# The opening re-planned with measured durations, and a tile's score stage joined to the preceding tile's output stage

## The chip, the cores and the metric

The kernel runs on one core of one Trainium2 chip. The metric is the time of one execution on the device in microseconds (us); of several runs the median is taken. The profile is one further execution, with its own time.

## The reference

Chunked attention, then two feed-forward layers over its output (4608 tokens of 512 features):

```python
def _attn_ref(q, k, v):                  # 8 x 8 x 576 x 64, chunks of 64
    scores = scale * np.matmul(q_c, k_c.transpose(0, 1, 2, 4, 3))
    scores = scores - np.max(scores, axis=-1, keepdims=True)
    attn = np.exp(scores)
    attn = attn / (np.sum(attn, axis=-1, keepdims=True) + 1e-09)
    out = np.matmul(attn, v_c)
def _moe_ref(x, w_in, w_out, alpha):     # 512 -> 2048 -> 512
    h = x @ w_in
    g = np.maximum(h, 0.0) + alpha * np.minimum(h, 0.0)
    return g @ w_out
def _moe2_ref(x, w_in, w_out):
    h = x @ w_in
    g = np.where(h > 0.0, h, np.exp(np.minimum(h, 0.0)) - 1.0)
    return g @ w_out
```

All inputs are float32; the weights are handed over as 64-bit words and are turned into float32 on the chip.

## The kernel before

The 4608 tokens are 9 blocks of 512, and a block is 4 attention tiles of 128 tokens (36 tiles, numbered t). Each float32 operand of the two layers is split into a high and a low part, and a product is three TensorE matmuls (high times high, high times low, low times high).

**A tile's attention** is three stages on TensorE, with work of other engines between them:
- S(t), `att_s` (L227): 16 matmuls for the scores, of q and the block-diagonal k (`kbd`). Behind it `softmax` on VectorE (maximum and subtraction, L238 and L240), `exponent` on ScalarE (L245), `normalize` on VectorE (L249 to L251) and `weigh` (L255; on VectorE for tiles 0 to 3, on GpSimd, POOL in the profile, for the others).
- T(t), `att_pt` (L266): 4 transposes of the weights `p`. Behind it `put_pt` (L272): two ScalarE copies into the block-diagonal buffer `pbd`, of which there is one.
- V(t), `att_av` (L280): 16 matmuls for the output of the tile, of v and `pbd`. Behind it `put_x` (L292), a ScalarE copy into `xf`; a block's four tiles are split into `xhi` and `xlo` (L342, L346; for block 0 L511 and L515).

The scores, the transposes and the outputs share two PSUM buffers (`ps_a`); in the first 12 stages the four accumulators of the second product serve too.

**A layer's step** is F(j,f), `first` (L366): 12 matmuls of 128x512 for slice f (of 16) of the hidden features of block j, into one of two PSUM buffers `h`; the activation and the split of its result follow on ScalarE and VectorE; and `second` (L438): 12 matmuls of 128x512 that add that slice into the accumulators `acc`.

**Three parts follow one another.** `start()`, the opening, plans tasks by a list scheduler: each task has an engine, a cost and a due time; of those whose predecessors are issued it takes the one that could begin first by its own sums, and among those within SLACK the one due first. What it takes is issued at once, so this sets the order of every engine's queue, SyncE's DMA queue (SP) among them. In the opening the weights are prepared piece by piece (32 pieces of the first layer: load, abs L125, low L150, clamp L132 and L136, join L143, add L155 on POOL, hi L159, lo L163 on POOL), tiles 0 to 11 are attended, and F(0,·), F(1,·) run, then F(2,·) in turn with second(0,·). Results g of blocks 0 to 2 are stored to memory (L569) and loaded again for `second`. MERGE is the number of slices of block 0 that come before F(1,0). `catch_up()` then runs the second product of blocks 1 and 2, and `rest()` the remaining blocks of the first layer and then all of the second layer: each step is one `first`, at most one attention stage of the next block, and one `second`. `att_order(j)` gives the stages of a block's four tiles in the order "S0 S1 T0 S2 V0 T1 S3 V1 T2 - V2 T3 - V3", one a step, "-" being a step without one. `att_stage` issues a stage; what follows it on other engines is put into `later` and issued by `flush()` at the next stage or `second`. The first layer ends near 920 us; behind that there is no attention left.

Of the kernel before, what the change touches and what calls it, by code (L numbers as in the profile page):

```python
# [22 lines left out]
START = 25.0  # L23
STEP = 3.6
LAG = 0.3
SLACK = 0.2
MERGE = 8
# [12 lines left out]
def tile_chunk_attention_prelu_elu(  # L40
# [420 lines left out]
    def start():  # L461
# [8 lines left out]
        def add(name, engine, cost, due, do, *after):  # L470
            def issue():
                got[name] = do()

            tasks[name] = (engine, cost, due, issue, after)
# [3 lines left out]
        for i in range(2 * KFF):  # L478
            name, f = ("in", "out")[i // KFF], i % KFF
            due = START + STEP * i - 6 if i < KFF else START + STEP * (KFF + f + 4)  # L480
            held_by = ()
            if name == "out" and f in held:
                held_by = (held[f],)
# [9 lines left out]
            add(("load", i), "dma", 1.5, due, w_load, ("add", i - 3))  # L493
            add(("abs", i), "act", 0.6, due, w_abs, ("load", i), ("lo", i - 2), ("add", i - 1))
            add(("low", i), "act", 0.6, due, w_low, ("abs", i))
            add(("clamp", i), "dve", 1.0, due, w_clamp, ("abs", i))
            add(("join", i), "dve", 0.8, due, w_join, ("clamp", i))
            add(("add", i), "pool", 1.3, due, w_add, ("join", i), ("low", i))
            add(("hi", i), "act", 0.6, due, hi, ("add", i), ("lo", i - 1), *held_by)
            add(("lo", i), "pool", 1.3, due, lo, ("hi", i))  # L500
# [3 lines left out]
        stages = [(int(op[1]), "STV".index(op[0])) for op in "S0 S1 T0 S2 V0 T1 S3 V1 T2 V2 T3 V3".split()]  # L504
        for j in range(1, AHEAD):
            stages += [op for op in att_order(j) if op]
# [10 lines left out]
        def user(n):  # L517
            t, k = stages[n]
            return (("max", t), ("put", t), ("y" if t < TPB else "x", t))[k]

        for n, (t, k) in enumerate(stages):
            j = t // TPB
            due = 4 + 2.5 * t if j == 0 else START + STEP * (KFF * (j - 1) + 3 * (t % TPB) + 1)
            free = n - (5 if n < 12 else 2)
            need = [user(free)] if free >= 0 else []
            need += [(("k", t),), (("weigh", t),), (("put", t), ("v", t))][k]
            if n:
                need.append(("STV"[stages[n - 1][1]], stages[n - 1][0]))
            bank = banks[n % 5] if n < 12 else banks[0]
            add(("STV"[k], t), "pe", (1.1, 0.5, 1.1)[k], due, lambda t=t, k=k, bank=bank: ATT[k][0](t, *bank), *need)  # L530
            if k == 0:
                add(("k", t), "dma", 1.5, due - 3, lambda t=t: load_qk(t), ("S" if place(t) == 0 else "V", t - PLACES))
                add(("v", t), "dma", 0.7, due, lambda t=t: load_v(t), ("V", t - PLACES), ("k", t))
                add(("max", t), "dve", 1.35, due, lambda t=t: softmax(t, got["S", t]), ("S", t), ("T", t - 2))
                add(("exp", t), "act", 0.55, due, lambda t=t: exponent(t), ("max", t))
                add(("norm", t), "dve", 1.1, due, lambda t=t: normalize(t), ("exp", t))
                add(("weigh", t), "dve" if j == 0 else "pool", 0.6 if j == 0 else 1.1, due, lambda t=t: weigh(t), ("norm", t))
            if k == 1:
                add(("put", t), "act", 1.0, due, lambda t=t: put_pt(t, got["T", t]), ("T", t), ("V", t - 1))
            if k == 2 and j == 0:  # L540
                add(("x", t), "act", 0.5, due, lambda t=t: x0(t), ("V", t))
                add(("y", t), "dve", 0.7, due, lambda t=t: y0(t), ("x", t))
            if k == 2 and j > 0:
                add(("x", t), "act", 0.5, due, lambda t=t: put_x(t, got["V", t]), ("V", t), *((("xhi", 1, kk) for kk in range(KDM)) if j == 2 else ()), *((("xlo", 1, kk) for kk in range(KDM)) if j == 2 else ()))
        n = AHEAD * TPB
        add(("k", n), "dma", 1.5, 1e3, lambda n=n: load_qk(n), ("S", n - PLACES))
        add(("v", n), "dma", 0.7, 1e3, lambda n=n: load_v(n), ("V", n - PLACES), ("k", n))
        for j in range(1, AHEAD):
            due = START + STEP * (KFF * j - 2)
# [3 lines left out]
            for kk in range(KDM):  # L553
                def x_first(j=j, kk=kk):
                    if kk == 0:
                        x_parts(1, j, spare=(j == 1))
                    x_hi(1, j, kk)

                add(("xhi", j, kk), "act", 0.55, due, x_first, *ready, ("xhi", j, kk - 1))
                add(("xlo", j, kk), "dve", 0.65, due, lambda j=j, kk=kk: x_lo(1, j, kk), ("xhi", j, kk))  # L560


        firsts = [(0, f) for f in range(KFF)]
        for f in range(KFF):
            firsts.insert(MERGE + 2 * f + 1, (1, f)) if MERGE + 2 * f + 1 < len(firsts) else firsts.append((1, f))
        firsts += [(2, f) for f in range(KFF)]
# [4 lines left out]
        for n, (j, f) in enumerate(firsts):  # L571
            due = START + STEP * n if j < 2 else START + STEP * 2 * KFF + 5.2 * f + 2.6
            ready = [("y", t) for t in range(TPB)] if j == 0 else [("xlo", j, kk) for kk in range(KDM)]
            before = [firsts[n - i] if n >= i else (9, 9) for i in range(4)]
            add(("F", j, f), "pe", 2.6, due, lambda j=j, f=f: first(1, j, f), *ready, ("lo", f), ("F", *before[1]), ("parts", *before[2]))
            last = ("store", *before[3 if j < 2 else 2])
            if j < 2:
                add(("parts", j, f), "act", 1.0, due + 3, lambda j=j, f=f: prelu_parts(got["F", j, f]), ("F", j, f), last)
                add(("join", j, f), "dve", 0.7, due + 3, lambda j=j, f=f: prelu_join(f, *got["parts", j, f]), ("parts", j, f))
                add(("store", j, f), "dma", 0.8, due + 3, lambda j=j, f=f: store(j, f, got["parts", j, f][0]), ("join", j, f))  # L580
            else:
                add(("parts", j, f), "dve", 1.4, due + 3, lambda f=f: prelu(f, got["F", 2, f]), ("F", j, f), last)
                add(("store", j, f), "dma", 0.8, due + 3, lambda f=f: store(2, f, got["parts", 2, f]), ("parts", j, f))
        for s in range(KFF + 3):
            j, f = divmod(s, KFF)
            due = START + STEP * 2 * KFF + 5.2 * s
            add(("g", s), "dma", 0.8, due - 12, lambda j=j, f=f: g_load(j, f), ("store", j, f), ("glo", s - 3))
            if s <= KFF:
                add(("ghi", s), "act", 0.55, due - 5, lambda j=j, f=f: g_hi(1, j, f, gl_t[j, f]), ("g", s), ("second", s - 3), ("store", 1, KFF - 1), ("glo", s - 1))
                add(("glo", s), "dve", 0.65, due - 5, lambda j=j, f=f: g_lo(1, j, f, gl_t.pop((j, f))), ("ghi", s))  # L590
            if s < KFF:
                add(("second", s), "pe", 2.6, due, lambda f=f: second(1, 0, f), ("glo", s), ("lo", KFF + f), ("second", s - 1))
        add(("alpha",), "dma", 0.1, 12, lambda: nc.sync.dma_start(out=alpha_sb, in_=alpha))
        add(("neg",), "dve", 0.1, START, lambda: nc.vector.tensor_scalar_mul(neg_alpha, alpha_sb, -1.0), ("alpha",))
        t = tasks["join", 0, 0]
        tasks["join", 0, 0] = (*t[:4], (*t[4], ("neg",)))

        done, free = {}, {}
        while tasks:
            best = None  # L600
            for name, (engine, cost, due, do, after) in tasks.items():
                if any(a in tasks for a in after):
                    continue
                at = max([free.get(engine, 0)] + [done.get(a, 0) + LAG for a in after])
# [6 lines left out]
            done[name] = at + cost + (2.0 if engine == "dma" else 0)  # L611
# [10 lines left out]
    def catch_up():  # L622
# [3 lines left out]
        for s in range(KFF, AHEAD * KFF):  # L626
            j, f = divmod(s, KFF)
            g_ahead(s)
            if s % 2 == 0 and stages:
                att_stage(stages.pop(0))  # L630
# [7 lines left out]
    def rest():  # L638
# [3 lines left out]
        for s, (ph, j, f) in enumerate(steps):  # L642
# [11 lines left out]
            if stages:  # L654
                att_stage(stages.pop(0))
# [62 lines left out]
```

## Time and profile before

| | |
|---|---|
| median of 3 runs | 1716.97 us (1716.6 to 1718.39) |
| the profiled execution, its own time | 1718.72 us |
| its span in the trace | 1716.9 us |
| TensorE (PE) busy | 1684.2 us, 98% |
| VectorE (DVE) / ScalarE (ACT) / GpSimd (POOL) busy | 864.9 / 551.3 / 214.7 us |
| mean granted TensorE clock | 0.995 of full speed |

The page cuts the span into 40 equal slices of 43 us and gives each engine's busy share in tenths; the first slices are the opening. The chain of waits goes back from the last instruction to what released each step. The timeline lists instructions in order of time with the idle time before each and the engine that ended it. PE's busy time counts a matmul from its start to a modelled end, and at half clock for as long as it then took; so a busy PE need not be at its peak.

### The profile page before, as it was taken

How to read it: one execution, taken by the hardware profiler on the slowest of the kernel's cores; microseconds unless marked ns; L12 is line 12 of the kernel's file. 1: busy time of each engine (PE TensorE's matmuls, PEld its weight loads, DVE VectorE, ACT ScalarE, POOL GpSimd, SP SyncE). 2: the span in 40 equal slices, each digit the busy share in tenths (PEclk: the TensorE clock that was granted, in tenths of full speed). 3: DMA queues.
4: the chain of work that ended last, by engine and by line, in shares of the span. 5: the costliest groups of instructions: out<-in, count | busy, mean ns of one | idle time of the engine just before them, and what ended most of it. 6: DMA issues, size and time to landing. Idle time of an engine off the chain costs nothing.

```text
span 1716.9 us, 20822 instructions
## 1 busy us (share of the span) xinstructions
PE 1684.2 (98%) x8208; PEld 1375.8 (80%) x8208; DVE 864.9 (50%) x1317; ACT 551.3 (32%) x937; POOL 214.7 (13%) x176
## 2 busy tenths in 40 slices
PE   6799999999999999999999999999999999999998
PEld 5587888888888888888887888888888888888887
DVE  6868743265655656564435343434343444444443
ACT  4776423222323233322233232322222222222222
POOL 3545410011110211110043000000000000000000
PEclk8999999999999999999999999999999999999999
DMA  7755544333323323320143010101010000000000
GB/s 227 216 171 191 178 134 137 92 123 99 111 93 124 115 76 123 99 86 20 50 129 117 1 49 1 50 0 50 1 45 5 34 16 27 23 19 31 12 14 25
DMA packets 72578, 133.48 MB, mean 78 GB/s; under 512 B 7328, under 2 KB 23712, under 8 KB 71328
## 3 DMA queue, kind: packets, MB, share of 16 engines
q1 hardware_dynamic: 72480, 132.16, 24.0%
q8 instruction: 64, 1.05, 0.3%
q14 instruction: 34, 0.28, 0.1%
HBM read 92.28 MB, written 39.85 MB: 77 GB/s over the span
## 4 chain that ended last, share of the span: by engine, by line
PE 94%; DVE 3%; ACT 1%; DMA 1%; issue 1%; SPq 0%; POOL 0%; DVEq 0%; ACTq 0%; POOLq 0%
PE acc L438 46%; PE h L366 43%; PE x L280 2%; PE s L227 2%; PE pt L266 1%; DVE xlo L346 1%; DVE pos L385 1%; DVE wt L132 0%; SPq L205 0%; ACT pbd L272 0%; DMA out<-k_t 0%; ACT wt L125 0%; DMA out<-q_t 0%; DMA q<-q_t 0%; DVE mx L238 0%
## 5 line engine op out<-in xcount | busy, mean ns | idle before, releaser
L366 PE MATMUL h<-xhi,in 128*128 128x512 f32 x2176 | 714.9, 391 | 2.9 <-POOL in L163 1.3
L366 PEld LDWEIGHTS h<-xhi,in 128*128 128x128 f32 x2176 | 409.2, 188 | 90.9 <-POOL in L163 2.4
L366 PE MATMUL h<-xlo,in 128*128 128x512 f32 x1088 | 424.5, 390 | 1.6 <-DVE xlo L346 1.4
L438 PE MATMUL acc<-ghi,out 128*128 128x512 f32 x1152 | 382.4, 396 | 0.0
L438 PE MATMUL acc<-out,ghi 128*128 128x512 f32 x1152 | 354.6, 389 | 0.0
L413 ACT ACTIVATE ghi<-gf 128x512 fp32r<-128x512 f32 x240 | 151.6, 632 | 481.6 <-DVE gf L394 364.1
L418 DVE TENSOR_TENSOR glo<-gf,ghi 128x512 fp32r<-128x512 f32 x240 | 166.3, 693 | 183.5 <-ACT ghi L413 183.5
L438 PEld LDWEIGHTS acc<-ghi,out 128*128 128x128 f32 x1152 | 216.2, 188 | 52.3 <-issue 8.2
L438 PEld LDWEIGHTS acc<-out,ghi 128*128 128x128 f32 x1152 | 216.2, 188 | 44.8
L366 PEld LDWEIGHTS h<-xlo,in 128*128 128x128 f32 x1088 | 204.8, 188 | 44.8 <-DVE xlo L346 2.9
L404 ACT ACTIVATE gf<-gf 128x512 f32<-128x512 f32 x144 | 91.0, 632 | 454.2 <-DVE gf L403 454.2
L438 PE MATMUL acc<-glo,out 128*128 128x512 f32 x576 | 224.8, 390 | 0.0
L438 PE MATMUL acc<-out,glo 128*128 128x512 f32 x576 | 224.1, 389 | 0.0
L403 DVE TENSOR_SCALAR gf<-h 128x512 f32<-128x512 f32 x144 | 99.4, 691 | 220.3 <-PE h L366 220.3
L391 DVE TENSOR_SCALAR gf<-h,alpha_sb 128x512 f32<-128x512 f32 x112 | 83.2, 743 | 146.8 <-PE h L366 146.8
L405 DVE SCALAR_TENSOR_TENSOR gf<-gf,h 128x512 f32<-128x512 f32 x144 | 99.2, 689 | 109.0 <-ACT gf L404 109.0
L155 POOL TENSOR_TENSOR wt<-wt,w 128x512 int32<-128x512 int32 x64 | 88.8, 1387 | 377.4 <-DVE wt L143 198.9
L438 PEld LDWEIGHTS acc<-out,glo 128*128 128x128 f32 x576 | 108.2, 188 | 22.5
L438 PEld LDWEIGHTS acc<-glo,out 128*128 128x128 f32 x576 | 108.3, 188 | 20.1
L394 DVE SCALAR_TENSOR_TENSOR gf<-h,gf 128x512 f32<-128x512 f32 x112 | 77.4, 691 | 3.8
L418 DVE TENSOR_TENSOR glo<-gl,ghi 128x512 fp32r<-128x512 f32 x48 | 35.7, 743 | 63.0 <-ACT ghi L413 63.0
L255 POOL TENSOR_TENSOR p<-p,sm 128x512 f32<-128x512 f32 x32 | 35.5, 1110 | 213.3 <-DVE sm L251 213.3
(60 smaller groups left out, 1023.2 us busy)
## 6 DMA issues: line engine op xcount, KB each, us to landing
w<-moe_w_in SPq DMA_DIRECT2D x32, 512.0 KB, 4.6
w<-moe_w_out SPq DMA_DIRECT2D x32, 512.0 KB, 3.8
gl<-g SPq DMA_DIRECT2D x48, 256.0 KB, 2.8
mid<-ost SPq DMA_DIRECT2D x36, 256.0 KB, 2.4
xf<-mid SPq DMA_DIRECT2D x9, 1024.0 KB, 5.1
out<-ost SPq DMA_DIRECT2D x36, 256.0 KB, 2.0
g<-pos SPq DMA_DIRECT2D x32, 256.0 KB, 2.7
kbd<-k_t SPq DMA_DIRECT2D x54, 128.0 KB, 2.7
```

What stands on the lines that cost most here:

```text
L155: nc.gpsimd.tensor_tensor(out=t, in0=t, in1=words[:, 0], op=ALU.add)
L227: nc.tensor.matmul(s[par * CH:(par + 1) * CH, hp], qq[:, h * CH:(h + 1) * CH], kbd[place(t)][:, :, h, :], start=True, stop=True,)
L255: (nc.vector if t < TPB else nc.gpsimd).tensor_tensor(out=p_t[t], in0=p_t[t], in1=sm, op=ALU.mult)
L366: nc.tensor.matmul(h, w[:, a], x, start=(kk == 0 and m == 0), stop=(kk == KDM - 1 and m == 2),)
L391: nc.vector.tensor_scalar(out=gf, in0=h, scalar1=0.0, scalar2=alpha_sb[:, f:f + 1], op0=ALU.min, op1=ALU.mult)
L394: nc.vector.scalar_tensor_tensor(out=gf, in0=h, scalar=0.0, in1=gf, op0=ALU.max, op1=ALU.add)
L403: nc.vector.tensor_scalar_min(gf, h, 0.0)
L404: nc.scalar.activation(out=gf, in_=gf, func=AF.Exp)
L405: nc.vector.scalar_tensor_tensor(out=gf, in0=gf, scalar=-1.0, in1=h, op0=ALU.add, op1=ALU.max)
L413: nc.scalar.activation(out=ghi, in_=gf, func=AF.Copy)
L418: nc.vector.tensor_sub(glo, gf, ghi.bitcast(F32))
L438: nc.tensor.matmul(acc[e], l, r, start=(f == 0 and m == 0), stop=(f == KFF - 1 and m == 2))
```

## The change

`COST` gives the planner a duration for each kind of task, in place of numbers beside each task; `START`, `STEP`, the lag and the due times of weights, loads and attention are new; the engines are free for planning at 2.0 (DMA queue), 6.5 (POOL) and 4.0. `MERGE` goes from 8 to 4. Tiles 4 to 7 are staged in the order of block 0, followed by S(8) (`ONE = 2`); from there `att_order` yields a list of stages for each step: T(t), then V(t) with S(t+1) directly behind it, then two steps without any. In the opening such a pair is one PE task (`run`), in `catch_up` and `rest` one call of `att_step`. So S(t+1), that of the next block too, stands in the step of V(t): 27 pairs, of V(8) with S(9) to V(34) with S(35), and S(12) moves from `catch_up` into the opening. What each engine computes is the same.

```diff
-START = 25.0
-STEP = 3.6
-LAG = 0.3
+COST = {
+    "load": 2.25, "k": 2.3, "v": 1.15, "store": 1.1, "g": 1.1, "alpha": 0.1,
+    "abs": 0.7, "low": 0.7, "clamp": 1.05, "wjoin": 0.75, "add": 1.35, "hi": 0.67, "lo": 1.35,
+    "S": 1.23, "T": 0.46, "V": 1.23, "VS": 2.15, "F": 2.72, "second": 2.72,
+    "max": 1.42, "exp": 0.67, "norm": 1.15, "weigh": 0.7, "weigh_pool": 1.3, "put": 1.22,
...
+LAG = 0.12
+LAND = 1.9
 SLACK = 0.2
-MERGE = 8
+START = 33.0
+STEP = 3.0
+
+MERGE = 4
+
+ONE = 2
...
     def att_order(j):
 
-        for op in "S0 S1 T0 S2 V0 T1 S3 V1 T2 - V2 T3 - V3".split():
-            yield (j * TPB + int(op[1]), "STV".index(op[0])) if op != "-" else None
+
+        for t in range(j * TPB, (j + 1) * TPB):
+            yield ((t, 1),)
+            yield ((t, 2), (t + 1, 0)) if t + 1 < NTILE else ((t, 2),)
+            yield ()
+            yield ()
...
-    def att_stage(stage):
-        if stage is None:
-            return
-        t, k = stage
-        pe, post = ATT[k]
-        while (t, k - 1) in later:
+    def att_step(ops):
+        while any((t, k - 1) in later for t, k in ops):
             flush()
-        got = pe(t, ps_a, "a")
+        got = [ATT[k][0](t, ps_a, "a") for t, k in ops]
         flush()
-        load_next(t, k)
-        later[t, k] = lambda: post(t, got)
+        for (t, k), o in zip(ops, got):
+            load_next(t, k)
+            later[t, k] = lambda t=t, k=k, o=o: ATT[k][1](t, o)
...
+        stages = []
+        for j in range(AHEAD):
+            if j < ONE:
+                ops = "S0 S1 T0 S2 V0 T1 S3 V1 T2 V2 T3 V3".split()
+                stages += [(j * TPB + int(op[1]), "STV".index(op[0])) for op in ops]
+                stages += [(ONE * TPB, 0)] * (j == ONE - 1)
+            else:
+                stages += [op for ops in att_order(j) for op in ops]
...
+        def run(units):
+            for n in units:
+                t, k = stages[n]
+                got["STV"[k], t] = ATT[k][0](t, *bank(n))
...
-        done, free = {}, {}
+        done, free = {}, {"dma": 2.0, "pool": 6.5}
```

**On TensorE in the opening, around S(8) and T(8).** Before, from V(7) on (`in_724` and `in_801` are the weights of slices 5 and 6, each F being nine rows):

```order
L280 MATMUL x<-pbd,out_423 64x128 x8
L227 MATMUL s<-kbd_93,q 64x128 x8
L366 MATMUL h<-xhi,in_724 128x512
...
L227 MATMUL s<-out_94,out_629 64x128 x8
L366 MATMUL h<-xhi,in_801 128x512
...
L266 MATMUL pt<-ident,p 128x128 x4
L227 MATMUL s<-out_95,out_711 64x128 x8
```

Now, from F(0,4) on (`in_674`; `in_381` is slice 0, which with `out_718` is F(1,0); `in_1060` slice 11, `in_853` slice 7, `in_1113` slice 12):

```order
L385 MATMUL h<-xhi,in_674 128x512
...
L245 MATMUL s<-kbd_93,q 64x128 x8
L385 MATMUL h<-out_718,in_381 128x512 x3
...
L385 MATMUL h<-xhi,in_1060 128x512
...
L284 MATMUL pt<-ident,p 128x128 x4
L385 MATMUL h<-out_718,in_853 128x512 x3
...
L298 MATMUL x<-pbd,v 64x128 x8
L245 MATMUL s<-out_94,out_634 64x128 x8
L385 MATMUL h<-xhi,in_1113 128x512
```

Between S(8) and T(8) stood two F and S(9); now there stand 14 F, and S(9) has moved behind V(8), with two F between it and T(9).

**On TensorE in `rest`, block 3.** Before, S and V each stand alone between a `first` (h) and a `second` (acc):

```order
L366 MATMUL h<-xhi,in_724 128x512
L227 MATMUL s<-kbd_93,q 64x128 x8
L438 MATMUL acc_3164<-ghi,out_1528 128x512
...
L366 MATMUL h<-xhi,in_801 128x512
L280 MATMUL x<-pbd,v 64x128 x8
L438 MATMUL acc_3164<-ghi,out_1578 128x512
```

Now:

```order
L284 MATMUL pt<-ident,p 128x128 x4
L457 MATMUL acc_3179<-ghi,out_1399 128x512
...
L385 MATMUL h<-xhi,in_613 128x512
L298 MATMUL x<-pbd,v 64x128 x8
L245 MATMUL s<-kbd_93,q 64x128 x8
L457 MATMUL acc_3179<-ghi,out_1504 128x512
```

V and S stand in one stretch, one step (a `second` and a `first`) behind the T of the same tile, where V used to follow its T after two steps.

## Rows read from the trace of the kernel before

**Rows 1.** The page: span, PE's busy line, granted clock in 40 slices, chain by engine

```profile
span 1716.9 us, 20822 instructions
...
PE 1684.2 (98%) x8208; PEld 1375.8 (80%) x8208; DVE 864.9 (50%) x1317; ACT 551.3 (32%) x937; POOL 214.7 (13%) x176
...
PEclk8999999999999999999999999999999999999999
...
PE 94%; DVE 3%; ACT 1%; DMA 1%; issue 1%; SPq 0%; POOL 0%; DVEq 0%; ACTq 0%; POOLq 0%
```

**Rows 2.** Who PE waited for, whole span: us in total, times, longest

```profile
PE s L227 <- DMA q<-q_t: 7.0, 2, 6.2
PE pt L266 <- DVE p L255: 5.8, 2, 4.2
PE pt L266 <- POOL p L255: 5.6, 2, 4.8
PE x L280 <- ACT pbd L272: 4.5, 5, 1.3
```

**Rows 3.** Chain by time, block 3: start us, us, what, count

```profile
352.93 1.02 PE s L227 x16
353.95 2.94 PE acc L438 x12
356.89 2.72 PE h L366 x12
...
378.92 1.02 PE x L280 x16
379.94 2.94 PE acc L438 x12
...
385.61 0.44 PE pt L266 x4
386.05 2.77 PE acc L438 x12
...
391.54 1.02 PE s L227 x16
```

**Rows 4.** Timeline of PE, V(7), S(8), T(8), S(10): start, us, what, count, idle before

```profile
60.69 1.09 PE L280 MATMUL x<-pbd,out 128*64 128x128 f32 x16
61.61 1.04 PE L227 MATMUL s<-kbd,q 128*64 128x128 f32 x16
62.59 0.50 PE L366 MATMUL h<-xhi,in 128*128 128x512 f32 x1
...
76.27 1.12 PE L266 MATMUL pt<-ident,p 128*128 128x128 f32 x4 [4.85 <-POOL p L255]
77.31 1.98 PE L227 MATMUL s<-out,out 128*64 128x128 f32 x16
```

**Rows 5.** Chain by time: F(0,7) at 79 us, and the first second(0,0)

```profile
79.29 4.45 PE h L366 x12
...
166.11 2.72 PE acc L438 x12
```

**Rows 6.** Windows: us, busy by engine, granted clock, DMA share, GB/s

```profile
57.00:85.00 28.00, 21.17 (x137) 15.53 (x136) 23.91 (x36) 18.28 (x34) 15.39 (x12) 0.88 0.70 214
```

**Rows 7.** Timeline of PE: waits at 163 and 252 us

```profile
163.10 0.50 PE L366 MATMUL h<-xhi,in 128*128 128x512 f32 x1 [0.95 <-DVE gf L394]
...
252.40 1.09 PE L227 MATMUL s<-kbd,q 128*64 128x128 f32 x16 [0.72 <-DMA q<-q_t]
```

**Rows 8.** Timeline of PE, S(6)

```profile
42.01 1.09 PE L227 MATMUL s<-out,out 128*64 128x128 f32 x16 [0.63 <-PE pt L266]
```

**Rows 9.** Timeline of POOL, weigh of tiles 6 and 8

```profile
46.63 1.29 POOL L255 TENSOR_TENSOR p<-p,sm 128x512 f32<-128x512 f32 x1 [2.62 <-DVE sm L251]
...
74.85 1.36 POOL L255 TENSOR_TENSOR p<-p,sm 128x512 f32<-128x512 f32 x1 [0.44 <-DVE sm L251]
```

**Rows 10.** Timeline of ScalarE, put_pt behind the T at 385.61

```profile
387.77 1.17 ACT L272 COPY pbd<-pt 64x512 f32<-64x512 f32 x2
```

More of the change, by code (lines that the diff above doesn't have):

```diff
@@ L468, in start, with add, task @@
         tasks, got = {}, {}
-        def add(name, engine, cost, due, do, *after):
+        def add(name, engine, due, do, *after, cost=None):
             def issue():
                 got[name] = do()
-            tasks[name] = (engine, cost, due, issue, after)
+            tasks[name] = (engine, COST[cost or name[0]], due, issue, after)
+        firsts = [(0, f) for f in range(KFF)]
+        for f in range(KFF):
+            firsts.insert(MERGE + 2 * f + 1, (1, f)) if MERGE + 2 * f + 1 < len(firsts) else firsts.append((1, f))
+        firsts += [(2, f) for f in range(KFF)]
+        f_due = {}
+        for n, (j, f) in enumerate(firsts):
+            f_due[j, f] = START + STEP * n if j < 2 else START + STEP * 2 * KFF + 5.44 * f + 2.72
+        f_due[AHEAD, 0] = START + STEP * 2 * KFF + 5.44 * KFF
+        s_due = [START + STEP * 2 * KFF + 5.44 * s for s in range(KFF + 3)]
+        stages = []
[6 more added lines that the diff above has]
+                stages += [op for ops in att_order(j) for op in ops]
+        def task(t, k):
+            return ("V", t - 1) if k == 0 and t > ONE * TPB else ("STV"[k], t)
         held = {6: ("S", 9), 7: ("S", 10), 8: ("S", 11), 9: ("V", 9), 10: ("V", 10), 11: ("V", 11)}
@@ L491, in lo, with bank, user @@
                 w_lo(wt[f"1{name}", f], single.pop(0)[4].bitcast(F32))
[L493 to L500, printed above, removed]
-        banks = [(ps_a, "a"), *((ps_acc, f"acc{e}") for e in range(KDM))]
-        stages = [(int(op[1]), "STV".index(op[0])) for op in "S0 S1 T0 S2 V0 T1 S3 V1 T2 V2 T3 V3".split()]
-        for j in range(1, AHEAD):
-            stages += [op for op in att_order(j) if op]
+            add(("load", i), "dma", due - LOAD_EARLY, w_load, ("add", i - 3))
+            add(("abs", i), "act", due, w_abs, ("load", i), ("lo", i - 2), ("add", i - 1))
+            add(("low", i), "act", due, w_low, ("abs", i))
+            add(("clamp", i), "dve", due, w_clamp, ("abs", i))
+            add(("wjoin", i), "dve", due, w_join, ("clamp", i))
+            add(("add", i), "pool", due, w_add, ("wjoin", i), ("low", i))
+            add(("hi", i), "act", due, hi, ("add", i), ("lo", i - 1), *held_by)
+            add(("lo", i), "pool", due, lo, ("hi", i))
+        banks = [(ps_a, "a"), *((ps_acc, f"acc{e}") for e in range(KDM))]
+        def bank(n):
+            return banks[n % 5] if n < 3 * TPB else banks[0]
+        def user(n):
+            t, k = stages[n]
+            return (("max", t), ("put", t), ("y" if t < TPB else "x", t))[k]
         parts0 = x_parts(1, 0)
@@ L515, in y0 @@
             nc.vector.tensor_sub(parts0[1][:, :, a], got["V", t], parts0[0][:, :, a].bitcast(F32))
-        def user(n):
-            t, k = stages[n]
-            return (("max", t), ("put", t), ("y" if t < TPB else "x", t))[k]
+        def run(units):
+            for n in units:
+                t, k = stages[n]
+                got["STV"[k], t] = ATT[k][0](t, *bank(n))
+            return got["STV"[stages[units[0]][1]], stages[units[0]][0]]
         for n, (t, k) in enumerate(stages):
             j = t // TPB
[L523 to L530, printed above, removed]
-            if k == 0:
[L532 to L537, printed above, removed]
@@ new lines, in start @@
+            due = 4 + 2.5 * t if j == 0 else f_due[j, 0] - ATT_EARLY[j] - ATT_STEP[j] * (TPB - t % TPB)
+            if task(t, k) == ("STV"[k], t):
+                units = [n] + [n + 1] * (n + 1 < len(stages) and task(*stages[n + 1]) == ("STV"[k], t))
+                need = [task(*stages[n - 1])] if n else []
+                for m in units:
+                    free = m - (5 if m < 3 * TPB else 2)
+                    if free >= 0:
+                        need.append(user(free))
+                    need += [[("k", stages[m][0])], [("weigh", t)], [("put", t), ("v", t)]][stages[m][1]]
+                add(task(t, k), "pe", due, lambda units=units: run(units), *need, cost="VS" if len(units) > 1 else None)
@@ new lines, in start @@
+            if k == 0:
+                if t < AHEAD * TPB:
+                    add(("k", t), "dma", due - 3, lambda t=t: load_qk(t), task(t - PLACES, 0 if place(t) == 0 else 2))
+                    add(("v", t), "dma", due, lambda t=t: load_v(t), ("V", t - PLACES), ("k", t))
+                add(("max", t), "dve", due, lambda t=t: softmax(t, got["S", t]), task(t, 0), ("T", t - 2))
+                add(("exp", t), "act", due, lambda t=t: exponent(t), ("max", t))
+                add(("norm", t), "dve", due, lambda t=t: normalize(t), ("exp", t))
+                on = "dve" if t < TPB else "pool"
+                add(("weigh", t), on, due, lambda t=t: weigh(t), ("norm", t), cost="weigh" if on == "dve" else "weigh_pool")
@@ L543, in start @@
+                add(("y", t), "dve", due, lambda t=t: y0(t), ("x", t))
             if k == 2 and j > 0:
[L544 to L547, printed above, removed]
+                parts = [(p, 1, kk) for p in ("xhi", "xlo") for kk in range(KDM)] if j == 2 else ()
@@ L557, in x_first @@
                     x_hi(1, j, kk)
[L559 to L566, printed above, removed]
+                add(("xhi", j, kk), "act", due, x_first, *ready, ("xhi", j, kk - 1))
+                add(("xlo", j, kk), "dve", due, lambda j=j, kk=kk: x_lo(1, j, kk), ("xhi", j, kk))
         def store(j, f, g):
@@ L591, in start @@
             if s < KFF:
[L592 to L596, printed above, removed]
-        done, free = {}, {}
+                add(("second", s), "pe", due, lambda f=f: second(1, 0, f), ("glo", s), ("lo", KFF + f), ("second", s - 1))
@@ L603, in start @@
                     continue
-                at = max([free.get(engine, 0)] + [done.get(a, 0) + LAG for a in after])
+                at = max([free.get(engine, 4.0)] + [done.get(a, 0) + LAG for a in after])
                 if best is None or at < best[0] - SLACK or (at < best[0] + SLACK and due < best[1]):
@@ L610, in start @@
             free[engine] = at + cost
-            done[name] = at + cost + (2.0 if engine == "dma" else 0)
+            done[name] = at + cost + (LAND if engine == "dma" else 0)
     def g_ahead(s):
@@ L629, in catch_up @@
             if s % 2 == 0 and stages:
-                att_stage(stages.pop(0))
+                att_step(stages.pop(0))
             if s == AHEAD * KFF - 2:
@@ L654, in rest @@
             if stages:
-                att_stage(stages.pop(0))
+                att_step(stages.pop(0))
             second(ph, j, f)
```

50 lines of the change are left out of this document (33 added, 17 removed).

## Prediction

> **What bounds the kernel now.** I read the page first: PE is busy for 98% of the span and the chain that ended last is PE for 94%, so the kernel is bound by TensorE, and only two things can shorten it: less time on PE for the same work, or fewer holes in its queue [rows 1]. The granted clock is 9 in every slice but the first, so time that is lost to the clock is lost in the opening [rows 1]. Then the waits of PE, to see where the holes are. Four kinds matter: S for the DMA of q, T for VectorE's `weigh`, T for POOL's `weigh`, V for `put_pt` on ScalarE; their longest are 6.2, 4.2, 4.8 and 1.3 us, and the totals are little more than those, so they are few and in the opening [rows 2]. Last the chain in a steady block, where nothing waits. There I read what a stage costs: a group of 12 big matmuls takes 2.72 us behind another group, but 2.94 behind an S or a V, and 2.77 behind a T [rows 3]. So an S or V of 1.02 us costs 1.24 in all, and a T of 0.44 costs 0.49.
>
> **The pairs.** The trace of before holds V and S side by side once at full clock, in the opening: V(7) begins at 60.69, S(8) at 61.61, the F behind them at 62.59 [rows 4]. V and S take 0.92 and 0.98 us, 1.90 together, and the F behind pays its 0.22 once. That is 2.12 against two times 1.24, which is 2.48: a pair saves 0.36 us. It is one row, so I bound it: if only the second toll goes, 0.22; nothing suggests more than 0.36, which I take. Pairs by the order: V(8) with S(9) to V(34) with S(35), 27, of which 4 stand in the opening and 23 behind it. The 23 give 23 x 0.36 = 8.3 us (5.1 at the low end). All stand on PE's path, since PE has no hole there; nothing covers them and nothing else must become faster.
>
> What the pairs move: V(t) used to stand two steps behind T(t) at most places and now stands one step behind. `put_pt` must fit in between. In the block read, T began at 385.61 and the place one step later, where S stands now, was 391.54 [rows 3]; `put_pt`'s two copies began at 387.77 and took 1.17, so they were done at 388.94 [rows 10]. That leaves 2.6 us: I cost it at 0.3 us in all, and if the cover went, V would wait as V waits in the opening, up to 1.3 us each [rows 2]. S(t+1) is earlier by itself four steps behind S(t), so its q and k have longer to land; the 0.72 us that S(13) waited for q at 252 us [rows 7] go. On SP the loads of q, k and v keep their order and are issued in the same steps as S and V, so no load is queued behind a later wait. T(t+1) is three steps behind S(t+1), over 16 us, far beyond what softmax and `weigh` need below.
>
> **The opening up to the end of S(8).** Both orders have done the same PE work when S(8) ends, before at 62.59 [rows 4]: 5 F at 2.72, 9 S and 8 V at 1.02, 8 T at 0.44, and about 1 us of tolls, together 35.5 us. From 6.2, when q had landed [rows 2], to 62.6 are 56.4, so some 21 us are lost: 5.8 to VectorE's `weigh`, 4.5 to `put_pt`, 0.8 of POOL's 5.6, and the rest for the most part to half clock and small weight waits. Of the 4.2 us that T(0) waited, the new order frees about half: on VectorE `weigh` of tile 0 now stands ahead of tile 1's maximum, and it stood behind tile 1's normalisation. The later T get part of this back, since the same VectorE work still lies ahead of `weigh` of tile 3. The V of tiles 1 to 3 still stand directly behind their T and keep their 1.3 each. The F come in another rhythm: S(5) ahead of F(0,0), F(0,1) directly behind F(0,0). On SP the weight loads of pieces 1 and 2 now stand behind loads that wait for V(0) and V(1); ScalarE doesn't reach piece 1 until about 10 us later, which covers a landing of 4 to 5 us. I take a gain of 2 us, with ends of -3 (T(3) or the first weights later, no T(0) gain kept) and +6 (half of the VectorE and `put_pt` waits and half the clock loss gone).
>
> **From S(8) to the first second(0,0).** Before, this took from 62.59 to 166.11 [rows 4, 5], 103.5 us. The work in it is 30 F (81.6), 3 S and 4 V (8.7) and 4 T (2.0), together 92.3. So 11.2 us are lost. 4.85 of them are T(8) waiting for POOL's `weigh`, and behind it PE ran at half clock: T(8) took 1.12, S(10) 1.98, F(0,7) 4.45 [rows 4, 5], from 76.27 to 83.74, 7.47 us for what takes 0.44 + 1.02 + 2.94 = 4.40 at full clock: 3.1 more. The granted clock of that stretch is 0.88 with PE idle for 6.8 of 28 us [rows 6]. 0.95 are a wait at 163 us for VectorE's activation [rows 7], and the other 2.3 small waits for weights.
>
> Now T(8) has 14 F behind S(8), some 38 us, where the road from S(8) to the end of `weigh` took 13.6 us before (62.65 to 76.21) [rows 4, 9]. So that wait and the half clock behind it go, 7.95 us. F(1,0) after four F instead of eight means that each weight piece serves two F, 5.44 us, from slice 5 on, so that weights have twice the time. The work now: 30 F (81.6), 4 T (2.0), 4 pairs at 2.12 (8.5), together 92.1, with S(12) in it, which costs `catch_up` 1.24 less.
>
> New waits here: T(9) and T(11) stand only two F, 0.22 + 5.44 us, behind their S. The road from S to the end of `weigh` was 4.8 us for tile 6 (S(6) ends at 43.10, POOL at 47.92) and 13.6 for tile 8, which stood in line with a second tile and the split of block 1 [rows 4, 8, 9]. T(9) and T(11) are alone, near the first: I take 1 us each, between 0 and 8 for the worse. Each of four V has only one F between it and its T; `put_pt` came 2.9 us after T's end in the row of block 3 [rows 3, 10] against 2.77 here: 0.5 in all. So 2.5 us of new loss, ends 0 and 9. The gain is 103.5 - 92.1 - 2.5 = 8.9 us.
>
> **The sum.** 2 + 8.9 (opening) + 1.24 + 0.72 (S(12) gone from `catch_up`, the wait for q) + 8.3 - 0.3 (23 pairs) = 20.9 us. The span was 1716.9, so 1696.0 now. The profiled execution's own time is 1718.72, 1.8 over its span; the median of the runs is 1716.97, which is the span within 0.1. So I forecast a median of **1696.0 us**.
>
> **Rivals.** (1) *The opening gains nothing.* ScalarE has two activations an F, the weights, and now tiles 8 to 11 in the same stretch, in one queue; T(9) to T(11) wait longer and the clock falls again. For it: VectorE is busy 23.9 of 28 us at 57 to 85 us [rows 6], so roads are long. Against it: with 14 F behind S(8), T(8) at least is safe. What is left are 27 pairs, 9.7, and 0.7: 1706.5 us. (2) *The pairs save nothing.* The mechanism would be that PE loads the next weights while the stage still runs, so that a group pays no toll wherever the stages stand; then the sum loses 27 x 0.36 = 9.7 and is 1705.7. Against it: 2.94 behind S or V and 2.72 otherwise, in every block [rows 3]. The Trainium skill says in "TensorE: Matmul & The Clock Gate", Part 2, "Step-by-step: what each phase is for", that PE's queue pulls weight loads ahead of running matmuls, so that the next tile's weights load while this one's run; by that rule there would be no toll to save. The trace doesn't agree behind these stages. (3) *V waits for `put_pt`,* the slower side. In `rest` ScalarE takes its queue in order, and `put_pt` stands behind the split of the activation, which waits for VectorE; with VectorE also at softmax and the second layer's weights, the 2.6 us of slack [rows 3, 10] would have to shrink by 3.7 us more. At 1.3 us for each of 23 V [rows 2] that is 30 us, 1726. It makes the kernel slower by more than 0.2% only from 1.06 us a V on ((1716.97 + 3.4 - 1696) / 23). VectorE would have to be late in every block; a steady block shows PE without a hole. (4) That the order doesn't do what it says is excluded: V and S stand side by side in it.
>
> **How the numbers follow.** Forecast 0.62 (1696; its own bounds: pairs 3 us less to none more, the first stretch 5 worse to 4 better, the second 6 worse to 2.5 better, which don't all fall together: 1690 to 1703); rival 1 0.24 (1703 to 1712), rival 2 0.06, rival 3 0.08. What this kernel's measurement can tell from no change is about 0.2%, 3.4 us. Rivals 1 and 2 still end faster, but for the far end of rival 1, 0.04. So faster 0.88, the same 0.04, slower 0.08. The range, with rival 3 and half of rival 1's far end left out, is 1689 to 1708.
>
> **What would show it.** In the trace of the changed kernel: in a steady block V and S together take 1.9 us and the group behind 2.94, and a block lasts 97.5 us instead of 99 (32 groups and four times 2.12 + 0.49). No 4.8 us wait of T for POOL, and no F of over 4 us near 80 us. second(0,0) begins near 158 us with one F more and S(12) behind it. Waits of T(9) and T(11) near 1 us. Wrong would make it: waits "x <- ACT pbd" in number after 170 us (rival 3), F of 4 us or a granted clock under 0.95 between 60 and 160 us (rival 1), or a group of 2.72 behind single stages or over 3.2 behind a pair (rival 2).

## The result and the profile after

The changed kernel takes 1703.46 us (median, 1702.88 to 1703.92), the kernel before 1717.68 in the same comparison; the ratio is 0.992 with an interval of 0.990 to 0.993. It is faster by 14 us. Forecast were 1696.0, 21 us faster, in a range of 1689 to 1708. So the way was right, the range held the time, and a third of the gain is missing.

The page of the kernel after, the lines that answer to [rows 1]:

```profile
span 1701.8 us, 20782 instructions
...
PE 1672.8 (98%) x8208; PEld 1377.1 (81%) x8208; DVE 866.7 (51%) x1317; ACT 552.9 (32%) x937; POOL 214.7 (13%) x176
...
PEclk8999999999999999999999999999999999999999
...
PE 95%; DVE 2%; ACT 1%; DMA 1%; issue 0%; POOL 0%; SPq 0%; DVEq 0%; ACTq 0%
```

PE works 11.4 us less and still fills 98%. The clock is again below full in the first slice alone.

A steady part of the first layer, the chain by time (start us, us, what, count), which answers to [rows 3]:

```profile
345.11 0.44 PE pt L284 x4
345.54 2.78 PE acc L457 x12
348.32 2.72 PE h L385 x12
351.04 1.02 PE x L298 x16
352.07 0.87 PE s L245 x16
352.94 2.94 PE acc L457 x12
...
369.49 0.44 PE pt L284 x4
```

V and S take 1.02 + 0.87 = 1.89 us, the group behind them pays its 0.22 once, and nothing waits. The four steps of a tile take 24.38 us (345.11 to 369.49).

Who PE waited for (us in total, times, longest), which answers to [rows 2]:

```profile
PE pt L284 <- DVE p L273: 8.1, 3, 4.1
PE s L245 <- DMA q<-q_t: 5.3, 1, 5.3
PE x L298 <- ACT pbd L290: 5.1, 5, 1.3
PE h L385 <- DVE xlo L365: 1.5, 2, 0.7
PE h L385 <- ACT neg L400: 1.4, 2, 1.1
PE pt L284 <- POOL in L181: 1.4, 1, 1.4
```

The 4.8 us wait of T for POOL's `weigh` is gone. V still waits for `put_pt` five times, as before, and all five are in the opening (the last at 55 us). But T waits 8.1 us for VectorE's `weigh`, 2.3 more than before, and F waits for ScalarE's activation, 1.4 us, which it didn't.

The opening, on the timeline of PE (start us, us, what, count, idle before):

```profile
11.45 1.09 PE L284 MATMUL pt<-ident,p 128*128 128x128 f32 x4 [1.73 <-DVE p L273]
...
18.74 1.97 PE L245 MATMUL s<-out,out 128*64 128x128 f32 x16
20.50 1.87 PE L298 MATMUL x<-pbd,out 128*64 128x128 f32 x16
...
29.44 1.12 PE L284 MATMUL pt<-ident,p 128*128 128x128 f32 x4 [4.06 <-DVE p L273]
...
63.35 1.09 PE L245 MATMUL s<-kbd,q 128*64 128x128 f32 x16
...
105.17 0.60 PE L284 MATMUL pt<-ident,p 128*128 128x128 f32 x4
...
115.95 0.60 PE L284 MATMUL pt<-ident,p 128*128 128x128 f32 x4
```

T(0) begins 3.1 us earlier than before (14.53 there); 0.9 of that is S(0)'s, as q had landed at 5.3 us in this execution and at 6.2 in that of before. T(3) begins 2.1 us later (27.30 there), and S(8), at 63.35, ends 1.8 us later than before [rows 4]. How far such a place moves between executions can be read from the experiments that leave the order up to it as it is: in the order of before S(8) begins at 61.61 and, with the pairs alone, at 62.18; in the changed order at 63.35, with the opening alone at 63.60, with the activations first at 64.40. So the loss is clear, but a single trace gives it only to about 1 us. T(8) and T(9), the last two rows, wait for nothing. Two stretches of the opening (us, busy by engine, granted clock, DMA share, GB/s), the second answering to [rows 6]:

```profile
13.00:33.00 20.00, 10.95 (x100) 9.39 (x98) 14.45 (x26) 10.90 (x19) 2.94 (x3) 0.81 0.72 217
...
57.00:85.00 28.00, 26.40 (x135) 20.20 (x133) 23.17 (x30) 19.93 (x38) 15.96 (x11) 1.00 0.68 209
```

From 57 to 85 us the clock is now full and PE idles 1.6 us instead of 6.8. From 13 to 33 it idles 9 of 20. Before, that stretch read:

```profile
13.00:33.00 20.00, 13.58 (x126) 11.52 (x128) 12.91 (x26) 11.05 (x19) 2.89 (x2) 0.79 0.78 254
```

It idled 6.4 there.

**The 14 us by place.** second(0,0) begins at 163.1 us instead of 166.1, with one F (2.7 us) more already done: the opening gives 5.7 us, of which S(8)'s end loses 1.8 and the stretch behind it gains 7.5. What follows gives 9.4. Together 15.1 us of span. In time it is 14 us: a run's time lies 1.8 us above its own span in both kernels, but the profiled execution of before took 1.0 us more than the median (1718.72 and 1717.68), that of the kernel after 0.1 (1703.57 and 1703.46).

### The profile page after: what moved, and what is told of

It is laid out like the page before. It is cut to its first block, busy times and chain, and to the rows that moved or that the text cites. A ratio compares the mean times of both kernels' runs of the same rounds, so it can differ in the third digit from the quotient of the medians.

```text
span 1701.8 us, 20782 instructions
## 1 busy us (share of the span) xinstructions
PE 1672.8 (98%) x8208; PEld 1377.1 (81%) x8208; DVE 866.7 (51%) x1317; ACT 552.9 (32%) x937; POOL 214.7 (13%) x176
## 4 chain that ended last, share of the span: by engine, by line
PE 95%; DVE 2%; ACT 1%; DMA 1%; issue 0%; POOL 0%; SPq 0%; DVEq 0%; ACTq 0%
PE acc L457 46%; PE h L385 44%; PE x L298 2%; PE s L245 2%; PE pt L284 1%; DVE xlo L365 0%; POOL wt L173 0%; DVE pos L404 0%; ACT pbd L290 0%; DMA out<-k_t 0%; DVE sm L267 0%; DVE p L258 0%; DVE mx L256 0%; DVE sm L268 0%; DMA q<-q_t 0%
## 5 line engine op out<-in xcount | busy, mean ns | idle before, releaser
L457 PE MATMUL acc<-ghi,out 128*128 128x512 f32 x1152 | 378.3, 394 | 0.0
L173 POOL TENSOR_TENSOR wt<-wt,w 128x512 int32<-128x512 int32 x64 | 88.9, 1388 | 335.6 <-issue 183.2
L273 POOL TENSOR_TENSOR p<-p,sm 128x512 f32<-128x512 f32 x32 | 36.3, 1133 | 261.6 <-DVE sm L269 261.1
L437 DVE TENSOR_TENSOR glo<-gl,ghi 128x512 fp32r<-128x512 f32 x48 | 42.2, 881 | 50.7 <-ACT ghi L432 50.7
```

The costliest lines, as they stand in the source:

```text
L173: nc.gpsimd.tensor_tensor(out=t, in0=t, in1=words[:, 0], op=ALU.add)
L273: (nc.vector if t < TPB else nc.gpsimd).tensor_tensor(out=p_t[t], in0=p_t[t], in1=sm, op=ALU.mult)
L437: nc.vector.tensor_sub(glo, gf, ghi.bitcast(F32))
L457: nc.tensor.matmul(acc[e], l, r, start=(f == 0 and m == 0), stop=(f == KFF - 1 and m == 2))
```

## Experiments

All differences of time are against the medians of the kernel before in the same comparison (1717.3 to 1717.7) or against the changed kernel's 1703.46.

**The pairs alone.** The opening of before, pairs behind it:

```diff
-        stages = list(att_order(AHEAD))
+        stages = [((AHEAD * TPB, 0),)] + list(att_pairs(AHEAD))
...
-                stages = list(att_order(j + 1))
+                stages = list(att_pairs(j + 1))
```

> The opening as before; S(12) alone at the start of the catch-up part, and behind it the 23 pairs V(12) with S(13) to V(34) with S(35). Theory (a pair saves the second toll and some of the joint, 0.36 us): 23 x 0.36 = 8.3 us less than before and the 0.72 us wait for q gone, so 9.0 less, some 1708 us; a block lasts 97.6 us instead of 99.0. Rival (the weights are loaded ahead, a pair saves nothing): only the 0.7 us, 1716.5 us. Rival (V waits for put_pt one step behind T): 1.3 us a V, some 30 us more.

Measured: 1709.43 us against 1717.51, 8.1 less, ratio 0.995 (0.994 to 0.997). Its chain has V with 1.02 and S with 0.87 in every tile, as above, and a tile takes 24.39 us (351.61 to 376.00), 97.6 for a block, as expected. V waits nowhere behind the opening. The wait of S(13) for q, 0.7 us, is gone here too, so that by the time alone 7.4 us are left for 23 pairs, 0.32 each. So a pair does save about what the single row of before said, and both the rival of the weights loaded ahead and that of `put_pt` fall.

**The opening alone.** The changed opening, then single stages:

```diff
+    def att_single(j):
+        for t in range(j * TPB, (j + 1) * TPB):
+            yield ((t, 1),)
+            yield ((t, 2),)
+            yield ((t + 1, 0),) if t + 1 < NTILE else ()
+            yield ()
```

> The changed opening; behind it T, V and S each in a step of its own (S one step behind V), so no pairs after the opening. Theory (the gains of the two parts add up): the changed kernel's 1703.5 plus 23 x 0.36 = 8.3, some 1711.8 us, and a block of 99.0 us. If the pairs were worth less than 0.36 it lies below 1711, and if the opening were worth nothing it lies near 1717.

Measured: 1711.98 us, 5.5 less than before (0.997, 0.996 to 0.998). Against the changed kernel it is 8.5 more, or 0.37 us for each of the 23 pairs. In its chain the four steps of a tile take 24.75 us, which is again 0.37 more than 24.38:

```profile
347.69 0.44 PE pt L284 x4
...
353.62 1.02 PE x L298 x16
354.64 2.94 PE acc L464 x12
...
360.31 1.02 PE s L245 x16
361.33 2.94 PE acc L464 x12
...
372.44 0.44 PE pt L284 x4
```

The two parts add up: 8.1 and 5.5 are 13.6 of the 14. (The 0.7 us of the wait for q are gone in both and so stand in this sum twice; the runs of one kernel lie 1 to 3 us apart, and the sum says no more than that nothing large is missing.) So the missing 7 us are the opening's, which I had put at 12.9 with S(12) and the wait for q, and which gave 5.5.

**Tile 3 first.** Why does T(3) wait 4 us? The VectorE rows of tile 3 in the changed kernel (L268 adds a constant, L273 is `weigh`), and POOL's beside them (L173 `add` and L181 `lo` of weight piece 0):

```profile
25.64 1.22 DVE L268 TENSOR_SCALAR sm<-sm 128x8 f32<-128x8 f32 x1
...
27.64 1.74 DVE L273 TENSOR_TENSOR p<-p,sm 128x512 f32<-128x512 f32 x1
```

```profile
25.55 1.28 POOL L173 TENSOR_TENSOR wt<-wt,w 128x512 int32<-128x512 int32 x1 [18.62 <-ACT w L168]
27.57 1.27 POOL L181 TENSOR_TENSOR in<-wt,in 128x512 fp32r<-128x512 f32 x1 [0.74 <-ACT in L177]
```

The add of 8 elements a partition takes 1.22 us and ends with POOL's instruction (26.86 and 26.83); before, with POOL idle, it took 0.17 (at 21.00 and at 24.52 us). The experiment takes tile 3 out of POOL's way:

```diff
+        move(('exp', 3), ('max', 3))
+        move(('norm', 3), ('exp', 3))
+        move(('weigh', 3), ('norm', 3))
```

(`move` puts a task's issue right behind another's; the plan is otherwise unchanged.)

> The changed kernel, but tile 3's exponent, normalisation and weighing are issued right behind its maximum and subtraction, ahead of weight piece 0 and of the split of tiles 1 and 2. Theory (T(3)'s 4.06 us wait comes from the place of tile 3 in the queues of ScalarE and VectorE, and from VectorE instructions of 1.2 and 1.7 us that run beside POOL's work on piece 0): T(3) begins some 3.5 us earlier (near 25.9 instead of 29.4), the VectorE add-constant of tile 3 takes 0.2 instead of 1.2 us and its multiply 0.7 instead of 1.7, and the span is 2.5 to 3.5 us shorter. Rival (the first F is held by the weight piece or the split, and T(3) is not on the road): F(0,0) begins within 0.5 us of 37.0 and the span is the same within 0.5 us.

Its VectorE, and its PE:

```profile
24.59 0.17 DVE L268 TENSOR_SCALAR sm<-sm 128x8 f32<-128x8 f32 x1
...
25.03 0.69 DVE L273 TENSOR_TENSOR p<-p,sm 128x512 f32<-128x512 f32 x1
```

```profile
26.13 1.98 PE L298 MATMUL x<-pbd,out 128*64 128x128 f32 x16 [2.75 <-ACT pbd L290]
28.03 1.12 PE L284 MATMUL pt<-ident,p 128*128 128x128 f32 x4
31.48 1.97 PE L298 MATMUL x<-pbd,out 128*64 128x128 f32 x16 [2.33 <-ACT pbd L290]
```

The slow instructions are short again, so they were POOL's doing. But T(3) is only 1.4 us earlier, not 3.5 (2.0 reckoned from S(0), which began 0.55 us later in this execution): V(2) now waits 2.75 us for `put_pt` of tile 2, which stands behind the exponent that was moved ahead, and V(3) 2.33 for that of tile 3, which stands behind weight pieces on ScalarE. V(3) begins 0.4 us earlier. The time is 1702.1, its interval (0.990 to 0.992) overlapping the changed kernel's. The wait was turned into another one; my theory had its place right and its worth wrong.

**A clock that stays up.** Matmuls on a tile of zeros, which nobody reads, in the idle places of TensorE:

```diff
+        def warm(n):
+            h = ps_h.tile([P, TB], F32, tag="h", name="hwarm")
+            for _ in range(n):
+                nc.tensor.matmul(h, warm_bf[:, 0:P], warm_bf[:, 0:TB], start=True, stop=True)
+
+        warm(10)
+        fill = {('S', 1): 6, ('V', 0): 8, ('T', 2): 4, ('V', 2): 12, ('T', 3): 4}
```

> The changed kernel with 44 added matmuls of 128x512 in bfloat16 on a tile of zeros, whose result nobody reads, in the idle places of TensorE in the opening: 10 ahead of S(0), 6 behind S(1), 8 behind V(0), 4 behind T(2), 12 behind V(2), 4 behind T(3). Theory (half clock in the opening is part of the shortfall: S, V and T up to 36 us took about double, and on the road to F(0,0) that is some 6.7 us): granted clock near 1.00 from 5 to 36 us, S(0) 1.1 us instead of 1.97, F(0,0) 4 to 6.5 us earlier than 37.0, and the span 3 to 6.5 us shorter. Rival (the road is VectorE's, so PE's speed there only lengthens its waits): stages at full clock but F(0,0) within 1 us of 37.0 and the span within 1 us. If the added matmuls delay stages instead, the span is longer by up to 3 us.

Measured: 1699.15 us, 4.3 less than the changed kernel, ratio to before 0.989 (0.988 to 0.991). From its windows and its timeline of PE:

```profile
13.00:33.00 20.00, 16.60 (x164) 10.74 (x159) 16.36 (x30) 13.06 (x22) 4.88 (x4) 1.00 0.73 219
```

```profile
12.25 1.09 PE L245 MATMUL s<-out,out 128*64 128x128 f32 x16
...
27.22 0.65 PE L284 MATMUL pt<-ident,p 128*128 128x128 f32 x4 [1.38 <-DVE p L273]
...
59.29 1.09 PE L245 MATMUL s<-kbd,q 128*64 128x128 f32 x16
```

The granted clock is 1.00 instead of 0.81, S(2) takes 1.09 instead of 1.98, T(3) is 2.2 us earlier, and S(8) ends 4.1 us earlier, which is the 4.3 of the time. Half clock is on the road.

**The same in the kernel before.** To see what the new order is worth when half clock is taken from both openings (`warm` as above, in that opening's own idle places):

```diff
+        fill = {('S', 1): 8, ('V', 0): 2, ('S', 3): 2, ('V', 1): 5, ('T', 2): 4, ('T', 3): 4, ('F', 0, 6): 14}
```

> The kernel before, with added matmuls on zeros in TensorE's idle places of its opening: 10 ahead of S(0), 8 behind S(1), 2 behind V(0), 2 behind S(3), 5 behind V(1), 4 each behind T(2) and T(3), 14 behind F(0,6). It tells what the new order is worth when neither opening runs at half clock. Theory (before, half clock cost about 3 us around T(8) and some 3 up to F(0,0)): 4 to 7 us shorter than before, 1711 to 1713 us. Then the new opening is worth 1699.2 + 8.3 (pairs) = 1707.5 against 1712, some 4.5 us, at full clock. Rival (VectorE sets the pace of that opening, and a faster TensorE waits longer): within 1.5 us of 1717.5, and the new order alone is worth 10 us at full clock.

Measured: 1713.89 us, 3.4 less than before (0.998, 0.997 to 0.999), a little under what I expected. From its timeline of PE and its windows:

```profile
59.12 1.04 PE L227 MATMUL s<-kbd,q 128*64 128x128 f32 x16
...
73.79 0.66 PE L266 MATMUL pt<-ident,p 128*128 128x128 f32 x4 [1.83 <-POOL p L255]
```

```profile
13.00:33.00 20.00, 17.57 (x156) 12.42 (x157) 14.25 (x26) 11.53 (x20) 4.20 (x3) 0.91 0.90 284
```

The clock of this opening is not quite full: it is 0.91 from 13 to 33 us, where S(2) took 1.52 and V(0) 1.97 us instead of 1.09, so 1.3 us of half clock are left in it. S(8) ends at 60.2 here and at 60.3 in the changed order with the same remedy. So up to S(8) the new order is worth nothing where the clock is held; without the last half clock the order of before might even be a little ahead. That the new order suffers more from half clock (S(8) ended 4.1 us later without the matmuls, against 2.5 before) rests on one trace each, whose places are good to about 1 us; in the times the matmuls gave 4.3 and 3.4 us. Over the whole opening the new order is worth 1713.9 - (1699.2 + 8.5) = 6.2 us with the matmuls in both, and 5.5 as the clock was; all of that comes from behind S(8).

**Activations first.** The 1.4 us of F waiting for ScalarE:

```diff
+        move(('exp', 8), ('parts', 1, 0))
+        move(('hi', 6), ('parts', 0, 5))
...
+        move(('abs', 7), ('lo', 6))
+        move(('low', 7), ('abs', 7))
```

> The changed kernel, with only two places of ScalarE's queue changed behind S(8): the activation of F(1,0) ahead of tile 8's exponent, and that of F(0,5) ahead of weight pieces 6 and 7. Theory (ScalarE's queue is taken in order, and the two waits of F for it, 1.11 and 0.26 us, come from an exponent that waits for VectorE and a weight piece that waits for POOL): F(0,6) begins 0.8 to 1.1 us earlier and the span is about 1 us shorter, 1702.4 us. Rival (F(0,6) is due for its weight piece at the same time): it then waits for POOL's low part of piece 6, and the time is the same within 0.5 us.

From its waits of PE:

```profile
PE h L385 <- POOL in L181: 1.2, 1, 1.2
...
PE h L385 <- ACT neg L400: 0.3, 1, 0.3
```

The wait for ScalarE goes and a wait of 1.2 us for the low part of a weight piece on POOL comes in its place; the time is 1703.31. The rival was right: F(0,6) was due for both at once.

**All three together.** Added matmuls, tile 3 first with `put_pt` of tiles 2 and 3 ahead of what stood before them, and the activations first:

```diff
+        move(('exp', 3), ('abs', 0))
...
+        move(('x', 1), ('put', 2))
+        move(('hi', 0), ('put', 3))
...
+        fill = {('S', 1): 6, ('V', 0): 6, ('T', 2): 4, ('T', 3): 4}
```

> The changed kernel with three things. (a) added matmuls on zeros in TensorE's idle places: 10 ahead of S(0), 6 behind S(1), 6 behind V(0), 4 each behind T(2) and T(3). (b) tile 3 first on all its queues: exponent, normalisation and weighing right behind its subtraction, put_pt of tile 2 ahead of the split of tile 1, put_pt of tile 3 ahead of weight pieces 0 and 1. (c) behind S(8), the activation of F(1,0) ahead of tile 8's exponent and that of F(0,5) ahead of weight pieces 6 and 7. Theory (clock and ScalarE's order add up): T(3) near 23.5 us instead of 27.2 with the matmuls alone, S(8) ends 2.5 to 4 us earlier than there, the 1.4 us of waits for ScalarE behind S(8) go; some 1695 us, 4 less than with the added matmuls alone. Rival (VectorE's and POOL's work from 26 to 58 us sets S(8)'s end): S(8) ends within 1 us of where it did, and only the 1.4 us are gained, 1697.7 us.

Measured: 1698.01 us, ratio to before 0.989 (0.987 to 0.991): 5.5 us under the changed kernel, and none of the other kernels that compute the whole of the reference is faster. It is near the rival's 1697.7, not the theory's 1695. From its timeline of PE:

```profile
22.54 0.66 PE L284 MATMUL pt<-ident,p 128*128 128x128 f32 x4
...
36.64 0.60 PE L284 MATMUL pt<-ident,p 128*128 128x128 f32 x4
...
57.95 1.09 PE L245 MATMUL s<-kbd,q 128*64 128x128 f32 x16
```

T(3), the first row, begins 4.7 us earlier than with the matmuls alone, as forecast, and S(8) still ends only 1.3 us earlier. Tile 4's T, the second row, has taken back nearly all of it: it began at 37.55 with the matmuls alone, 0.9 us later. So up to S(8) it isn't TensorE's own road alone that sets the pace.

**What else sets the pace.** Two experiments on that stretch, in the kernel with all three things:

```diff
-        (nc.vector if t < TPB else nc.gpsimd).tensor_tensor(out=p_t[t], in0=p_t[t], in1=sm, op=ALU.mult)
+        (nc.vector if t < 2 * TPB else nc.gpsimd).tensor_tensor(out=p_t[t], in0=p_t[t], in1=sm, op=ALU.mult)
```

> The kernel with all three things, with `weigh` of tiles 4 to 7 on VectorE instead of POOL (0.6 us each there instead of 1.1 to 1.3). If POOL is what is late, S(8) ends 1 to 2 us earlier, 1696.5 us. If VectorE is (26.9 of 32 us busy from 26 to 58 us), its 2.4 us more are late in place of POOL's, and the time is the same or up to 1.5 us longer. If neither is on the road, nothing changes.

Measured: 1698.09, the same. T(4) comes 1.9 us earlier (34.77), but T(5) then waits 2.8 us, by the trace for tile 4's `put_x` on ScalarE, the clock of the stretch from 26 to 58 us is lower (0.89 against 0.95), and S(8) begins at 59.02, 1.1 us later. What POOL gave up came back in that wait for ScalarE.

```diff
+        if TPB <= t < 2 * TPB:
+            return
```

(in `weigh`, ahead of the multiplication; these tiles are then not divided by their sums, and the run only prices that work)

> The kernel with all three things (added matmuls, tile 3 first, activations first), without the four multiplications of `weigh` of tiles 4 to 7 on POOL; so the outputs of those tiles are left undivided by their sums. It prices POOL's share of the stretch that ends with S(8). Theory (VectorE and POOL set the pace of 26 to 58 us; four POOL multiplications of 1.1 to 1.3 us and the VectorE instructions that run longer beside them lie on the road): S(8) ends 2 to 4 us earlier than 59.0, about 1695 us. Rival (the road there is ScalarE's and the weights' own chain, and POOL has room): S(8) ends within 0.7 us of 59.0, and the time is 1698 within 0.7.

Measured: 1696.56, S(8) begins at 56.45 and ends 1.5 us earlier than with that work; between the two expectations. POOL's four multiplications are worth 1.5 us of the time; what the rest of that stretch hangs on, VectorE, ScalarE or the weights' own chain, isn't taken apart here.

## Why the prediction was right and where it wasn't

**The pairs: right, from one row.** Forecast 0.36 us each from V(7) and S(8) [rows 4]; measured 0.37 (24.75 against 24.38 us a tile in the chain, 1711.98 against 1703.46 in time), 1.02 + 0.87 in the chain. Behind a stage a group takes 2.94 against 2.72 in both kernels, so rival 2 is out. Where the toll lies is seen in the timeline of the changed kernel, with the weight loads (PEld) beside the matmuls:

```profile
352.87 0.19 PEld L457 LDWEIGHTS acc<-ghi,out 128*128 128x128 f32 x1 [0.17 <-issue]
352.87 0.50 PE L457 MATMUL acc<-ghi,out 128*128 128x512 f32 x1
...
355.50 0.19 PEld L385 LDWEIGHTS h<-xhi,in 128*128 128x128 f32 x1
355.72 0.39 PE L385 MATMUL h<-xhi,in 128*128 128x512 f32 x1
```

Between two big groups the load begins 0.22 us before its matmul (355.50 and 355.72). Behind S it begins together with it (352.87), and this matmul takes 0.50 us instead of 0.39: half of the toll. The other half, about 0.1 us, lies ahead of the stage, whose own first load comes after 0.35 us without any. The rule of the Trainium skill that was named with rival 2 ("TensorE: Matmul & The Clock Gate", Part 2, "Step-by-step: what each phase is for") doesn't describe these places: there the load of the next weights isn't hidden whole. Why it isn't, no run here shows.

**`put_pt` one step behind T: right.** No V waits in any block; 0.3 us were set aside. The wait of S(13) for q is gone.

**From S(8) to second(0,0): right in kind, 1.4 us too good.** T(8)'s wait and the half clock behind it went (clock 1.00 from 57 to 85 us, F near 80 us at 2.9). The two waits that I priced, T(9) and T(11) at 1 us each, didn't come. Others did: F for ScalarE's activation 1.4, for the split of block 1 0.2, for VectorE's activation 0.6. Another 1.7 us are not waits by the profile's count, but nearly all of them stand beside these: an F before or behind one of the waits takes 2.87 to 2.90 us without the wait instead of 2.72 (from 70.51 to 74.50 it is 3.99, with a wait of 1.11), and F(1,0), behind S(8) and with a wait in its middle, 3.15; with 0.29 over the three F ahead of the wait at 160 us these make some 1.5. So a wait cost some 0.3 us more than its own length, a toll like that of the stages, which the prediction left out. (F(1,0) stands behind five F of block 0, and stood behind nine before: one more than the prediction says, in both kernels.) The mechanism of rival 1, ScalarE's queue taken in order, was there with 1.4 us. But the experiment shows it was no cost of its own, since F(0,6) would have waited for its weight 1.2 us in any case.

**Up to the end of S(8): wrong by 3.8 us.** This is the term that failed: "Of the 4.2 us that T(0) waited, the new order frees about half" and "I take a gain of 2 us". The first of these held: T(0) waited 1.73 us, and from S(0)'s start to T(0)'s it took 6.13 instead of 8.28. But nothing of it lasted, and S(8) ended 1.8 us later. With the clock held, or nearly, the two orders end S(8) at the same time, 60.2 and 60.3, so the 2 us had no ground even there. The likely reason is that VectorE, POOL and ScalarE had the same work between T(0) and S(8); the run in which T(3) came 4.7 us earlier and S(8) 1.3 points that way, but which of their steps take an earlier start back isn't shown. How much of the 1.8 us of loss half clock made stays open too. S(3) and V(1) ran at it (1.97 and 1.87 us), the 1.2 GHz level, where before they took 1.09 each, and from 13 to 33 us PE was busy 11.0 of 20 us instead of 13.6, partly because T(3) waited 4.1 us; yet the granted clock of that stretch was 0.81, and 0.79 before. I named half clock as a loss of before and gave it only a good end in the bounds; I didn't ask what the new order would do to the clock. Of the place I said that T(3) could be late, at the end of -3; it was -1.8.

**Behind the opening: right, 9.4 of 10.0 us. The relation of time to span: 1.7 us off.** A run's time lies 1.8 us over its own span, before (1718.72 and 1716.9) as after (1703.57 and 1701.8). I took the median to be the span, which held by chance: the profiled execution of before was itself 1.75 us over the median of the three runs. For an execution like that one the sum gives 1718.72 - 20.9 = 1697.8. 3.8 + 1.4 + 0.6 + 1.7 are the 7.5 us between 1696.0 and 1703.46.

## What to carry to other kernels

Where a small stage costs a toll in the group behind it, look for the one place in the trace where two such stages already stand side by side: that row said 0.36 us a pair, and the chain measured 0.37. An earlier start of one step in a chain can be worth little (4.7 us at T(3) gave 1.3 at S(8)): add up the work of the other engines between it and the next meeting point first, then move. A wait can cost more than its own length, as the groups before and behind it last longer too. In a stretch where TensorE waits, ask of the new order whether it keeps the clock: filling the waits with matmuls that nobody reads gave nearly as much here (4.3 us) as re-planning the whole opening (5.5).

## What was not expected of the hardware

VectorE's instructions beside POOL's: the add-constant on 128x8 took 1.22 us beside a POOL `tensor_tensor` and ended 0.03 us behind it, and 0.17 us when POOL was idle; a VectorE multiply of two operands in SBUF that began 0.07 us behind a POOL instruction took 1.74 instead of 0.69. The Trainium skill has this in "SBUF — State Buffer", "Who interferes with whom": VectorE's second port pair is shared with GpSimd, and where a VectorE instruction in a 2-port mode (a `tensor_scalar` can be), or one with two SBUF inputs, meets a GpSimd instruction that reads SBUF, the one that comes second is blocked until the first is done. The rows here agree with it, down to the 8-element add; that this add runs in a 2-port mode is not shown.

The granted clock can be held by matmuls on zeros: 1.00 from 13 to 33 us with 44 of them, 0.81 without, in the same order of the real work. With 30 of them it was 0.92 in one trace (all three together) and 1.00 in another (`weigh` on VectorE), and without any it ranged from 0.75 to 0.86 over three traces of the changed order.
